# Where ScalarE's read of a finished MLP tile stands among the exponentials of its visit

## The chip, the cores and the metric

The kernel runs on one core of a Trainium2 chip. The metric is the device time of one execution in microseconds (us), and the median of several executions counts. The core has five engines with a queue of their own each: TensorE (PE in the profile, with PEld for its weight loads) for matrix products, VectorE (DVE), ScalarE (ACT), GpSimd (POOL), and SyncE (SP), which here starts the DMA transfers. Each engine takes its instructions in the order in which they were issued to it, and waits on semaphores for the others.

## The reference

One transformer-like block in fp32 with 2048 tokens, 512 features, 32 heads of 16 and an MLP of width 1792:

```python
xn = _layernorm(x, axis=-1)
qkv = (xn @ wqkv).reshape(B, S, 3, H, Dh).transpose(2, 0, 3, 1, 4)
scores = jnp.einsum("bhqd,bhkd->bhqk", q, k) * (Dh ** -0.5)
p = softmax(scores, axis=-1)
s = jnp.einsum("bhqk,bhkd->bhqd", p, v).transpose(0, 2, 1, 3).reshape(B, S, D) @ wo
h = jnp.einsum("bsd,df->bsf", xn, w1) + b1
r = jnp.where(h > 0, h, 0)
m = jnp.einsum("bsf,fd->bsd", r * r, w2) + b2
return x + s * silu(m)
```

## The kernel before

After a lead-in (layer norm, the q, k and v projections) the kernel runs one loop of 512 *steps*. A step is one unit (four heads, 512 queries; 32 units) and one block of 128 keys (16 a unit). For a step TensorE makes four score tiles `se` of 128x512, ScalarE takes the exponential of each (`exp_mm`, lines 1161 and 1167), and two steps later four matmuls multiply them with v into `po` (`pv_mm`, line 374). The softmax needs a maximum of each row beforehand; it comes from a second set of score matmuls (`max_mm`, line 300), whose tiles `pm_t` VectorE reduces (line 308).

Products with a contraction of 64 or less use half of TensorE's rows. The kernel therefore has two *lanes*: lane 0 is rows 0 to 63, lane 1 rows 64 to 127, and matmuls of different lanes run side by side. The score and maximum matmuls belong to one lane or the other; the v matmuls use all the rows and a quarter of the columns each.

The MLP and the projection by wo are spread over the steps as "dense" work, on TensorE by line 234 (`block`) or line 202 (`halves`). Each is a sum of matmuls, hi and lo parts of both factors, into one PSUM tile `pd_t`. There is a single buffer of that tile (pool `pd`, `bufs=1`). So the first matmul of the next dense tile waits until the last reader of this one is through: ScalarE's two `Relu` of 128x256 for a pair of first-layer tiles (`first_pair`, line 545), or ScalarE's copy of 128x512 to `u` for the second layer (`second`, line 566). This closing read is called `post` in the code. Behind the Relu, GpSimd squares and splits (lines 548, 80, 81).

Each long dense tile, a *block*, is laid over four steps by `long_slots`. Its sums are cut into 12 units "D" for each lane; a unit is two matmuls of 256 columns in the first layer (`per=2`, input `xc`, weights `w1s`) and one of 512 in the second (`w2t`, `hT`). First lane 0 does its 12 units (h = 0, two steps), then lane 1 (h = 1, two steps), and meanwhile the other lane makes maxima ("m") and scores ("s"). `visit(h, mine, theirs)` takes both strings letter by letter: `mine` is lane h, `theirs` the other lane. Where the maxima are far enough ahead (`ahead_m`), a half is a single visit of 14 letters, followed by the v matmuls of two steps. Otherwise the half is split: ten D beside `msmsmsmsms`, the v matmuls of one step, then the short closing visit, `DDss` beside `mmsm`, and the v matmuls of another step. `post` is called behind the last visit of h = 1.

The program built from this has 88 blocks. In 54, all in the earlier part, both halves are single visits; in 34, all in the later part, both are split. 55 blocks end in a `post` (49 pairs of Relu, 6 copies): 34 of single visits and 21 of split ones. Of the 34 split blocks 19 are of the first layer.

The order of the work on each engine is that of the Python calls (`manual_schedule`): nothing reorders it. One further dependency is written out by hand: `last_use` is the exponential of the first score tile of lane h behind the lane's last D; the other lane's first D waits for it (line 239), since both lanes add into the same `pd_t`. The score tiles rotate over three PSUM buffers (`pe`, `bufs=3`), the maxima over three (`pm`). GpSimd's tile `r` has two buffers.

Of the kernel before, what the change touches and what calls it, by code (L numbers as in the profile page):

```python
# [39 lines left out]
def kernel(  # L40
# [55 lines left out]
    with ExitStack() as ph:  # L96
# [191 lines left out]
        def max_mm(j, spread=False):  # L288
            if not m_ready(j, 1):
                return None  # L290
            u, p, qb, kc = todo_m[j].pop(0)
            qd = u // 4
            if u not in mxs:
                mxs[u] = sp.tile([P, 16, 4], F32, name="mx")
            m_bank[0] += 1
            if spread and m_bank[0] % 2:
                ps = pe.tile([P, 512], F32, name="se")
            else:
                ps = pm.tile([P, 512], F32, name="pm_t")
            nc.tensor.matmul(  # L300
                ps,
                qms[u][p][64 * j : 64 * j + 64, qb * P : (qb + 1) * P],
                kas[qd, p][64 * j : 64 * j + 64, kc * 512 : (kc + 1) * 512],
                start=True, stop=True,
            )
            c = (2 * p + j) * 4 + qb
            done_m[j] += 1
            return nc.vector.tensor_reduce(  # L308
                mxs[u][:, c, kc : kc + 1], ps, axis=AX.X, op=ALU.max
            )  # L310
# [3 lines left out]
        def max_end():  # L314
            while steps[0] < sum(done_m) // 4:
                u, s = divmod(steps[0], 16)
                if s == 15 and min(done_m) < 32 * (u + 1):
                    return
                steps[0] += 1
                if s in (9, 11) and u + 1 < NU:  # L320
                    assert min(done_m) >= 32 * u + 16
                    load_q_pair(u + 1, "qm", (s - 9) // 2, qms.setdefault(u + 1, []))
                if s == 15:
                    m4 = sp.tile([P, 16], F32, name="m4")
                    nc.vector.tensor_reduce(m4, mxs[u], axis=AX.X, op=ALU.max)
                    mxs[u] = m4
                    late.append((now[0] + 2, u))

        def shift_due():
            if late and late[0][0] <= now[0]:  # L330
                shift(late.pop(0)[1])
# [821 lines left out]
        def exp_mm(st, j, pts, spare):  # L1153
            u, kb = divmod(st, 16)
            qd = u // 4
            b = 64 * (j % 2)
            if spare:
                se = pm.tile([P, 512], F32, name="pm_t")
            else:
                se = pe.tile([P, 512], F32, name="se")  # L1160
            nc.tensor.matmul(  # L1161
                se, kas[qd, j // 2][b : b + 64, kb * P : (kb + 1) * P],
                qes[u][j // 2][b : b + 64, :],
                start=True, stop=True,
            )
            pts[j] = free_pt.pop(0)
            return nc.scalar.activation(pts[j], se, AF.Exp, scale=0.25)  # L1167
# [3 lines left out]
        def pv_step(st, pts):  # L1171
            u, kb = divmod(st, 16)
            if kb == 0:
                pos[0] = pv.tile([P, 512], F32, name="po")
            pv_mm(pos[0], u // 4, kb, pts)
            free_pt.extend(t for _, t in sorted(pts.items()) if all(t is not x for x in gone_pt))
            if kb == NT - 1:
                if u < NU - 2:
                    evac(pos[0], u)
                elif u == NU - 2:  # L1180
                    unit_inner(pos[0])
                else:
                    unit_final(pos[0])
# [57 lines left out]
        def ahead_m(n, st):  # L1241
            wo0 = 16 * NU - 62
            for u in range(n // 64, NU):
                end = 16 * u - SHIFT
                n_max = n + 4 * max(0, end - st)
                n_max += max(0, min(end, wo0 + 32) - max(st, wo0))
                if n_max < 64 * (u + 1):
                    return False
            return True

        def long_slots(st0, units, post):

            todo = [[(st0 + k, j) for k in range(4) for j in (lane, lane + 2)] for lane in range(2)]
            for kb in range(st0, st0 + 4):
                pts.setdefault(kb, {})

            def s(lane):
                kb, j = todo[lane].pop(0)
                return exp_mm(kb, j, pts[kb], False)

            def visit(h, mine, theirs):
                own, other, follow = units[h], 1 - h, True
                for i, ops in enumerate(zip(mine, theirs)):
                    for lane in (other, h):
                        o = ops[0] if lane == h else ops[1]
                        if o == "D":
                            own.pop(0)()
                        elif o == "m":
                            max_mm(lane)
                        elif o == "s":  # L1270
                            use = s(lane)
                            if lane == h and not own and follow:
                                last_use[0], follow = use, False

            for h in range(2):
                st = st0 + 2 * h
                if st > st0:
                    begin(st)
                if ahead_m(sum(done_m) + 7, st + 2):
                    visit(h, "s" + "D" * 12 + "s", ".mmsmssmsmssmm")  # L1280
                    if h and post is not None:
                        post()
                    begin(st + 1)
                    max_end()
                    shift_due()
                    for kb in (st - 2, st - 1):
                        pv_step(kb, pts.pop(kb))
                else:
                    visit(h, "D" * 10, "msmsmsmsms")
                    max_end()  # L1290
                    shift_due()
                    pv_step(st - 2, pts.pop(st - 2))
                    begin(st + 1)
                    visit(h, "DDss", "mmsm")
                    if h and post is not None:
                        post()
                    max_end()
                    shift_due()
                    pv_step(st - 1, pts.pop(st - 1))
            if post is not None:  # L1300
                last_use[0] = None
            assert not todo[0] and not todo[1] and not units[0] and not units[1]
# [17 lines left out]
        def begin(st):  # L1320
            now[0] = st
            if st % 64 == 48 and st // 64 + 1 < NQ:
                load_v(st // 64 + 1)
            if st >= 64 and st % 64 < 6 and st // 64 + 1 < NQ:
                for n in range(2):
                    load_k(st // 64 + 1, 2 * (st % 64) + n)
            u, s = divmod(st + 16, 16)
            if 2 <= u < NU and s < 2:
                load_q_pair(u, "qe", s, qes.setdefault(u, []))
            run_waiting()  # L1330

        done = 0
        for st_ in range(NU * 16):
            if st_ < done:
                continue
            begin(st_)
            if st_ < 2:
                slot(st_, [], None, 6)
                shift_due()
                continue  # L1340
            if st_ == 2:
                assert len(rest) == 1 and next(rest[0], None) is None
                qs.close()
            item = next(dn, None)
            if item is not None and len(item) > 2:
                assert st_ % 4 == 0
                long_slots(st_, *item[:2])
                done = st_ + 4
                continue
            if item is not None and item[0] is not None:  # L1350
                slot(st_, *item)
            else:
                plain_slot(st_)
            shift_due()
            if st_ > 1:
                pv_step(st_ - 2, pts.pop(st_ - 2))
# [30 lines left out]
```

## Time and profile before

| what | value |
|---|---|
| median of 3 runs | 1714.3 us (1711.1 to 1719.36) |
| profiled execution, its own time | 1710.34 us |
| span in its trace | 1708.6 us |
| granted TensorE clock | 0.998 |
| TensorE busy | 1655.0 us, 97% |
| VectorE busy | 1337.6 us, 78% |
| ScalarE busy | 1193.0 us, 70% |
| GpSimd busy | 528.9 us, 31% |

The profiled execution took 4.0 us less than the median, and its span is 1.7 us shorter than its own time. In the rows of a group, the first numbers behind the bar are busy time and mean length of one instruction, then the idle time of the engine just before them and who ended it. In a timeline a row has the start (us), the time it covers, the engine, the line and the operation, the output and the inputs, the number of instructions run together (x), and in brackets the idle time of the engine before it with its releaser. Rows run together overlap: three exponentials of 0.61 us each can cover 1.57 us. 64*128 64x512 is a matmul on 64 rows of TensorE (one lane) that streams 512 columns.

### The profile page before, as it was taken

The page shows a single profiled execution, that of the slowest core. Times are in us where ns is not written, and L with a number is a line of the kernel's source. Part 1 is how long each engine was busy: PE and PEld are TensorE (multiplying, and loading weights), DVE is VectorE, ACT ScalarE, POOL GpSimd, SP SyncE. Part 2 cuts the span into 40 slices and gives each one's busy share as a digit, 9 for nine tenths or more (in the row PEclk, how much of TensorE's full clock was granted, in tenths as well). Part 3 has the DMA queues.
Part 4 walks back from the last instruction along what each step waited for, and adds up shares of the span by engine and source line. Part 5 has one row for each costly group of instructions (what it writes and reads, how often), then busy time and mean ns, then how long its engine had stood idle before and what let it go on. Part 6 is the DMA issues. An engine that isn't in the chain of part 4 may idle for free.

```text
span 1708.6 us, 35413 instructions
## 1 busy us (share of the span) xinstructions
PE 1655.0 (97%) x13296; PEld 987.1 (58%) x13296; DVE 1337.6 (78%) x2294; ACT 1193.0 (70%) x2354; POOL 528.9 (31%) x548
## 2 busy tenths in 40 slices
PE   6999999999999999999999999999999999999997
PEld 5766666556656655665566565545554555555533
DVE  6599988887787787788787878888888888888612
ACT  6211377778777777787787777777777777766685
POOL 4434467513212221232032122212220223133333
PEclk9999999999999999999999999999999999999999
DMA  7567454436233522353144234242324332157344
GB/s 278 167 202 245 171 174 157 133 84 163 77 87 94 138 73 79 119 131 93 52 142 103 88 87 116 64 110 85 101 70 119 88 104 57 40 190 210 100 144 136
DMA packets 156723, 208.00 MB, mean 122 GB/s; under 512 B 51272, under 2 KB 71240, under 8 KB 155016
## 3 DMA queue, kind: packets, MB, share of 16 engines
q1 hardware_dynamic: 156552, 205.74, 41.5%
q8 instruction: 105, 1.72, 0.4%
q14 instruction: 66, 0.54, 0.1%
HBM read 149.30 MB, written 56.09 MB: 120 GB/s over the span
## 4 chain that ended last, share of the span: by engine, by line
PE 82%; issue 5%; ACT 3%; POOL 3%; DMA 3%; DVE 2%; SPq 1%; POOLq 0%; ACTq 0%; DVEq 0%
PE po L374 24%; PE pd_t L234 15%; PE pm_t L300 14%; PE se L1161 13%; PE pd_t L202 6%; PE pd_t L936 2%; PE po L936 2%; DVE mx L308 2%; ACT pt L1167 2%; PE se L300 2%; ACT r L545 1%; PE po L967 1%; PE pd_t L967 1%; POOL ts L751 1%; POOL ts L750 1%
## 5 line engine op out<-in xcount | busy, mean ns | idle before, releaser
L308 DVE TENSOR_REDUCE mx<-pm_t 128x1 f32<-128x512 f32 x1946 | 1209.5, 683 | 251.8 <-PE pm_t L300 156.5
L1167 ACT ACTIVATE pt<-se 128x512 f32<-128x512 f32 x1721 | 909.5, 612 | 283.3 <-PE se L1161 185.0
L1161 PE MATMUL se<-qe,ka 64*128 64x512 f32 x1988 | 761.3, 421 | 2.0 <-ACT ex L1167 1.0
L300 PE MATMUL pm_t<-ka,qm 64*128 64x512 f32 x1946 | 737.4, 416 | 3.5 <-DVE mx L308 2.4
L374 PE MATMUL po<-pt,v 128*32 128x512 f32 x3562 | 522.2, 602 | 0.0
L300 PEld LDWEIGHTS pm_t<-ka,qm 64*128 64x128 f32 x1946 | 341.3, 184 | 220.7 <-DVE mx L308 202.3
L1161 PEld LDWEIGHTS se<-qe,ka 64*128 64x128 f32 x1988 | 352.9, 184 | 129.3 <-ACT pt L1167 57.1
L234 PE MATMUL pd_t<-xc,w1s 64*128 64x256 f32 x2352 | 317.9, 285 | 12.5 <-ACT r L545 11.5
L234 PEld LDWEIGHTS pd_t<-xc,w1s 64*128 64x128 f32 x2352 | 296.5, 187 | 20.9 <-ACT r L545 16.5
L234 PE MATMUL pd_t<-w2t,hT 64*128 64x512 f32 x936 | 248.1, 402 | 2.4 <-ACT r L545 2.4
L374 PE MATMUL po<-ex,v 128*32 128x512 f32 x534 | 204.8, 601 | 0.0
L1167 ACT ACTIVATE ex<-se 128x512 f32<-128x512 f32 x267 | 158.1, 612 | 51.0 <-PE se L1161 25.8
L374 PEld LDWEIGHTS po<-pt,v 128*32 128x32 f32 x3562 | 90.7, 108 | 157.4 <-issue 140.2
L234 PEld LDWEIGHTS pd_t<-w2t,hT 64*128 64x128 f32 x936 | 162.5, 184 | 11.5 <-issue 3.3
L548 POOL TENSOR_TENSOR r<-r 128x512 f32<-128x512 f32 x49 | 51.0, 1040 | 354.2 <-ACT r L545 354.2
L567 POOL TENSOR_TENSOR u<-u,b_t 128x512 f32<-128x512 f32 x16 | 20.6, 1287 | 290.8 <-ACT u L566 290.8
L202 PE MATMUL pd_t<-w2t,hT 64*128 64x512 f32 x408 | 105.8, 391 | 0.1
L412 POOL TENSOR_TENSOR ot<-ot,hl 128x512 f32<-128x512 f32 x31 | 39.8, 1283 | 199.1 <-DMA hl<-r_d 167.5
L202 PE MATMUL pd_t<-wot,oc 64*128 64x512 f32 x336 | 90.9, 406 | 8.7 <-DVE mx L308 6.2
L202 PEld LDWEIGHTS pd_t<-wot,oc 64*128 64x128 f32 x336 | 58.4, 184 | 58.7 <-ACT pt L1167 16.0
L308 DVE TENSOR_REDUCE mx<-se 128x1 f32<-128x512 f32 x102 | 69.7, 683 | 14.7 <-PE se L300 8.7
L202 PEld LDWEIGHTS pd_t<-w2t,hT 64*128 64x128 f32 x408 | 72.5, 184 | 9.8 <-POOL w2t L81 0.5
(125 smaller groups left out, 1229.5 us busy)
## 6 DMA issues: line engine op xcount, KB each, us to landing
w1s<-w_d SPq DMA_DIRECT2D x196, 256.0 KB
qm<-q_d SPq DMA_DIRECT2D x384, 32.0 KB
qe<-q_d SPq DMA_DIRECT2D x384, 32.0 KB
ka<-k_d SPq DMA_DIRECT2D x96, 128.0 KB
xn_d<-xT SPq DMA_DIRECT2D x8, 1024.0 KB
k_d<-hl SPq DMA_DIRECT2D x32, 256.0 KB
q_d<-hl SPq DMA_DIRECT2D x32, 256.0 KB
xc<-xn_d SPq DMA_DIRECT2D x16, 512.0 KB
```

The costliest lines, as they stand in the source:

```text
L202: mm = nc.tensor.matmul(out_, lh(r), rh(r), start=first_ and lane == 0, stop=last_ and lane == 1, skip_group_check=True,)
L234: mm = nc.tensor.matmul(out_, lh(r), rh(r), start=first_ and lane == 0, stop=last_ and lane == 1, skip_group_check=True,)
L300: nc.tensor.matmul(ps, qms[u][p][64 * j : 64 * j + 64, qb * P : (qb + 1) * P], kas[qd, p][64 * j : 64 * j + 64, kc * 512 : (kc + 1) * 512] ...
L308: return nc.vector.tensor_reduce(mxs[u][:, c, kc : kc + 1], ps, axis=AX.X, op=ALU.max)
L374: nc.tensor.matmul(po[32 * j : 32 * j + 32, :], vs[qd][:, (4 * kb + j) * VW : (4 * kb + j) * VW + 32], pts[j], start=(kb == 0), stop=(kb = ...
L412: nc.gpsimd.tensor_tensor(ot, ot, hl[:, 1].bitcast(F32), op=ALU.mult)
L548: nc.gpsimd.tensor_tensor(r, r, r, op=ALU.mult)
L567: nc.gpsimd.tensor_tensor(u, u, b2_t, op=ALU.add)
L936: nc.tensor.matmul(out_, lh(slice(0, P)), rh(slice(0, P)), start=first_, stop=last_)
L967: nc.tensor.matmul(out_, lh(slice(0, P)), rh(slice(0, P)), start=first_, stop=last_)
L1161: nc.tensor.matmul(se, kas[qd, j // 2][b : b + 64, kb * P : (kb + 1) * P], qes[u][j // 2][b : b + 64, :], start=True, stop=True,)
L1167: return nc.scalar.activation(pts[j], se, AF.Exp, scale=0.25)
```

## The change

`visit` gets a flag that lets lane h go first at each letter, used for the short closing visit of both halves; and `post` is no longer called behind the visit but inside it, at the letter at which lane 1 has issued its last D.

```diff
-            def visit(h, mine, theirs):
+            def visit(h, mine, theirs, h_first=False):
                 own, other, follow = units[h], 1 - h, True
                 for i, ops in enumerate(zip(mine, theirs)):
-                    for lane in (other, h):
+                    for lane in (h, other) if h_first else (other, h):
                         o = ops[0] if lane == h else ops[1]
...
+                    if h and not units[h] and wrap:
+                        wrap.pop()()
+
+            wrap = [post] if post is not None else []
             for h in range(2):
...
                     visit(h, "s" + "D" * 12 + "s", ".mmsmssmsmssmm")
-                    if h and post is not None:
-                        post()
                     begin(st + 1)
...
-                    visit(h, "DDss", "mmsm")
-                    if h and post is not None:
-                        post()
+                    visit(h, "DDss", "mmsm", True)
                     max_end()
```

The number and the kind of instructions are the same. On VectorE, GpSimd and SyncE no instruction moves; on TensorE and ScalarE some do. TensorE, the closing visit of h = 1 of a split first-layer block, from the v matmuls to the v matmuls; `ka0` with `qm0` is a maximum of the other lane, `se` a score tile. Before:

```order
L374 MATMUL po_19006<-pt4_1345,v0_1437 32x512
L300 MATMUL pm_t_19378<-ka0_203,qm0_200 128x512
L234 MATMUL pd_t_19225<-xc_17586,w1s3_2323 128x256 x2
L300 MATMUL pm_t_19383<-ka0_203,qm0_200 128x512
L234 MATMUL pd_t_19225<-xc_17586,w1s3_2323 128x256 x2
L1161 MATMUL se_19389<-qe3_689,ka1_204 128x512
L1161 MATMUL se_19392<-qe2_688,ka0_203 128x512
L300 MATMUL pm_t_19395<-ka0_203,qm0_200 128x512
L1161 MATMUL se_19398<-qe3_689,ka1_204 128x512
L374 MATMUL po_19006<-pt7_1348,v0_1437 32x512
```

The same visit with the change:

```order
L374 MATMUL po_19006<-pt7_1348,v0_1437 32x512
L234 MATMUL pd_t_19225<-xc_17586,w1s3_2323 128x256 x2
L300 MATMUL pm_t_19380<-ka0_203,qm0_200 128x512
L234 MATMUL pd_t_19225<-xc_17586,w1s3_2323 128x256 x2
L300 MATMUL pm_t_19386<-ka0_203,qm0_200 128x512
L1161 MATMUL se_19394<-qe2_688,ka0_203 128x512
L1161 MATMUL se_19397<-qe3_689,ka1_204 128x512
L1161 MATMUL se_19400<-qe3_689,ka1_204 128x512
L300 MATMUL pm_t_19403<-ka0_203,qm0_200 128x512
L374 MATMUL po_19006<-pt0_1341,v0_1437 32x512
```

Each pair of letters has changed places: D now stands ahead of the maximum beside it, and the lane's own score ahead of the other's. This happens in the closing visits of both halves of the 34 split blocks, 68 in all. ScalarE, the end of the same block; `r1<-pd_t_19225` are the two Relu that read it, `se_19416` is the first score tile of the next block. Before:

```order
L1167 ACTIVATE pt6_1347<-se_19365 128x512
L1167 ACTIVATE pt5_1346<-se_19389 128x512
L1167 ACTIVATE pt8_1349<-se_19392 128x512
L1167 ACTIVATE pt1_1342<-se_19398 128x512
L545 ACTIVATE r1_2312<-pd_t_19225,b1_t_148 128x256 x2
L1167 ACTIVATE pt11_1352<-se_19416 128x512
```

With the change:

```order
L1167 ACTIVATE pt10_1351<-se_19365 128x512
L545 ACTIVATE r1_2312<-pd_t_19225,b1_t_148 128x256 x2
L1167 ACTIVATE pt1_1342<-se_19394 128x512
L1167 ACTIVATE pt4_1345<-se_19397 128x512
L1167 ACTIVATE ex0_2305<-se_19400 128x512
L1167 ACTIVATE pt9_1350<-se_19416 128x512
```

The Relu pair has moved ahead of the three exponentials of the closing visit. In a block of single visits it moves ahead of one, and TensorE's order stays. ScalarE at the end of such a block, before:

```order
L1167 ACTIVATE pt6_1347<-se_7994 128x512
L1167 ACTIVATE pt12_1353<-se_8008 128x512
L545 ACTIVATE r0_2311<-pd_t_7855,b1_t_148 128x256 x2
L1167 ACTIVATE pt7_1348<-se_8029 128x512
L1167 ACTIVATE ex1_2306<-se_8042 128x512
```

With the change:

```order
L1167 ACTIVATE pt6_1347<-se_7994 128x512
L545 ACTIVATE r0_2311<-pd_t_7855,b1_t_148 128x256 x2
L1167 ACTIVATE pt12_1353<-se_8013 128x512
L1167 ACTIVATE pt7_1348<-se_8029 128x512
L1167 ACTIVATE ex1_2306<-se_8042 128x512
```

Only the exponential of the visit's last letter has changed sides with the Relu pair.

## The prediction

> **What bounds the kernel now.** I read the page first: the span, the engines and the chain of work that ended last.
>
> ```profile
> span 1708.6 us, 35413 instructions
> ...
> PE 1655.0 (97%) x13296; PEld 987.1 (58%) x13296; DVE 1337.6 (78%) x2294; ACT 1193.0 (70%) x2354; POOL 528.9 (31%) x548
> ...
> PE 82%; issue 5%; ACT 3%; POOL 3%; DMA 3%; DVE 2%; SPq 1%; POOLq 0%; ACTq 0%; DVEq 0%
> ```
>
> TensorE carries the end, so what an edit on ScalarE is worth is what it takes out of TensorE's waits. The view of the waits for TensorE alone has two rows on the first matmul of a dense tile, and the view of the groups tells which kind of D waited.
>
> ```profile
> PE pd_t L234 <- ACT r L545: 13.9, 19, 0.8
> ...
> PE pd_t L234 <- ACT u L566: 1.0, 2, 0.5
> ```
>
> ```profile
> L234 PE MATMUL pd_t<-xc,w1s 64*128 64x256 f32 x2352 | 317.9, 285 | 12.5 <-ACT r L545 11.5 <-ACT u L566 1.0
> ...
> L234 PE MATMUL pd_t<-w2t,hT 64*128 64x512 f32 x936 | 248.1, 402 | 2.4 <-ACT r L545 2.4
> ```
>
> Those are 19 + 2 = 21 waits, exactly the number of split blocks that end in a read; the 34 reads behind single visits have none. The groups divide them: 11.5 us of 0.72 each are 16 waits of a first-layer D for the Relu, 2.4 of 0.81 are 3 of a second-layer D, and 1.0 are the two for the copy (one wait of each size stands below). The 14.9 us that the two rows add up to are only the part in which TensorE did nothing at all; the timeline around one of them shows what a wait costs. First the end of a split block with its closing visit and the next block's first half, then, without a read ahead of it, that block's second half:
>
> ```profile
> 1200.39 0.49 PE L300 MATMUL pm_t<-ka,qm 64*128 64x512 f32 x1
> 1200.39 0.50 PE L234 MATMUL pd_t<-xc,w1s 64*128 64x256 f32 x2
> ...
> 1200.73 0.40 PE L234 MATMUL pd_t<-xc,w1s 64*128 64x256 f32 x2
> ...
> 1200.92 1.89 DVE L308 TENSOR_REDUCE mx<-pm_t 128x1 f32<-128x512 f32 x3 [0.50 <-PE pd_t L234]
> 1200.96 0.41 PE L1161 MATMUL se<-qe,ka 64*128 64x512 f32 x2
> ...
> 1201.19 0.32 SPq L468 DMA_DIRECT2D w1s<-w_d  x1
> ...
> 1201.39 1.57 ACT L1167 ACTIVATE pt<-se 128x512 f32<-128x512 f32 x3 [1.23 <-PE se L1161]
> ...
> 1201.53 1.07 PE L374 MATMUL po<-pt,v 128*32 128x512 f32 x8
> ...
> 1202.52 0.50 PE L300 MATMUL pm_t<-ka,qm 64*128 64x512 f32 x1
> 1202.83 0.85 ACT L545 ACTIVATE r<-pd_t,b_t 128x256 f32<-128x256 f32 x2
> ...
> 1203.74 0.38 PE L234 MATMUL pd_t<-xc,w1s 64*128 64x256 f32 x1 [0.72 <-ACT r L545]
> ...
> 1203.84 0.46 PE L1161 MATMUL se<-qe,ka 64*128 64x512 f32 x1
> ...
> 1206.32 0.62 PE L374 MATMUL po<-pt,v 128*32 128x512 f32 x2
> ...
> 1209.45 0.50 PE L234 MATMUL pd_t<-xc,w1s 64*128 64x256 f32 x2
> ...
> 1209.79 0.39 PE L1161 MATMUL se<-qe,ka 64*128 64x512 f32 x1
> ...
> 1209.98 3.08 DVE L308 TENSOR_REDUCE mx<-pm_t 128x1 f32<-128x512 f32 x5 [0.25 <-PE pm_t L300]
> ...
> 1210.71 0.39 PE L1161 MATMUL se<-qe,ka 64*128 64x512 f32 x1
> ...
> 1212.02 1.06 PE L374 MATMUL po<-pt,v 128*32 128x512 f32 x8
> ```
>
> The three exponentials start at 1201.39 behind 1.23 us of idling, then come the two Relu, which end at 1202.83 + 0.85 = 1203.68; the next block's first D starts 0.06 later, at 1203.74. Its visit had begun at 1202.52 with the other lane's maximum. Nothing behind that D in TensorE's queue could start, so the visit stood for 1203.74 - 1202.52 = **1.22 us**. From D to the v matmuls the visit then takes 1206.32 - 1203.74 = 2.58 us; in the half without a read it takes 1212.02 - 1209.45 = 2.57. Hence the wait isn't made up later: it lengthens the block by itself.
>
> **Part one: the read moves ahead of the exponentials, in split blocks.** The last D of the visit ends at 1200.73 + 0.40 = 1201.13. ScalarE has been idle since 1201.39 - 1.23 = 1200.16. With the change the Relu pair starts at about 1201.19 (the same 0.06 for the hand-over), takes 0.85 and ends at 1202.04. TensorE can't come to the next D before 1202.52. So the read is ready 0.48 us early and the whole wait goes. This is the first of the three kinds, with 16 waits. The other two, each with the start of its visit and the D:
>
> ```profile
> 1253.40 0.50 PE L300 MATMUL pm_t<-ka,qm 64*128 64x512 f32 x1
> ...
> 1254.71 0.47 PE L234 MATMUL pd_t<-w2t,hT 64*128 64x512 f32 x1 [0.81 <-ACT r L545]
> ```
>
> ```profile
> 1164.48 0.50 PE L300 MATMUL pm_t<-ka,qm 64*128 64x512 f32 x1
> ...
> 1165.47 0.38 PE L234 MATMUL pd_t<-xc,w1s 64*128 64x256 f32 x1 [0.50 <-ACT u L566]
> ```
>
> They cost 1.31 and 0.99. Sum: 16 x 1.22 + 3 x 1.31 + 2 x 0.99 = 19.5 + 3.9 + 2.0 = **25.4 us**.
>
> What is late next? The three exponentials now start at 1202.04 and end at 1203.61. Their score buffers are wanted by the next visit's scores: in the half without a wait these start 0.34 behind the visit's start (1209.79 - 1209.45) and then 0.46 apart ((1210.71 - 1209.79) / 2). From 1202.52 that is 1202.86, 1203.32 and 1203.78. The three exponentials, some 0.5 apart and 0.6 long, are through at about 1202.65, 1203.1 and 1203.6: 0.2 us to spare each time. I charge nothing; without this margin each lacking tenth would cost 21 x 0.1 = 2.1 us. The maxima do not come to bind either: in the half without a read VectorE idles 0.25 before its five reductions, waiting for TensorE. The transfer of weights issued at 1201.19 is for the block after the next (eight buffers, four a block), which can't begin before the second half at 1209.45: 8 us of slack.
>
> **Part two: the read moves ahead of one exponential, in blocks of single visits.** One such end, with the half before it, which has no read:
>
> ```profile
> 544.77 0.63 PE L374 MATMUL po<-pt,v 128*32 128x512 f32 x3
> ...
> 546.62 0.49 PE L1161 MATMUL se<-qe,ka 64*128 64x512 f32 x1
> ```
>
> ```profile
> 549.66 0.40 PE L234 MATMUL pd_t<-xc,w1s 64*128 64x256 f32 x2
> ...
> 550.23 1.92 PE L374 MATMUL po<-pt,v 128*32 128x512 f32 x16
> ...
> 550.57 0.66 ACT L1167 ACTIVATE pt<-se 128x512 f32<-128x512 f32 x1
> ...
> 551.04 0.90 ACT L545 ACTIVATE r<-pd_t,b_t 128x256 f32<-128x256 f32 x2
> ...
> 552.09 0.49 PE L1161 MATMUL se<-qe,ka 64*128 64x512 f32 x1
> ...
> 553.12 0.39 PE L1161 MATMUL se<-qe,ka 64*128 64x512 f32 x1
> ```
>
> Sixteen v matmuls lie between the last D and the next block. They take 552.09 - 550.23 = 1.86 us with a read in this time and 546.62 - 544.77 = 1.85 without, so the read, over at 551.94, is hidden and there is nothing to gain. The displaced exponential ends some 0.9 later than before, near 552.1. Its buffer is wanted by the third score of the next block, at 553.12. The margin is 1.0 us, and the cost of these 34 moves is nothing; without the margin it would be up to 0.9 each.
>
> **Part three: lane h goes first in 68 closing visits.** A first-layer D is two matmuls in one lane, and the other lane's maximum now stands behind both. Rows that show such an order are those where a block starts with D after a wait; the program has D, D, score there:
>
> ```profile
> 1412.08 0.38 PE L234 MATMUL pd_t<-xc,w1s 64*128 64x256 f32 x1 [0.71 <-ACT r L545]
> ...
> 1412.08 0.50 PE L1161 MATMUL se<-qe,ka 64*128 64x512 f32 x1
> ...
> 1412.30 0.40 PE L234 MATMUL pd_t<-xc,w1s 64*128 64x256 f32 x2
> ```
>
> The other lane's score starts with the first D, 0.22 ahead of the second, which it follows in the program: a lane doesn't wait for the other's second matmul. At the other start shown the score came 0.10 behind the D (1203.84 against 1203.74), still ahead of its second matmul. So a visit loses between 0 and 0.10, 0 to 6.8 us over 68; a gain is excluded, since no matmul is taken away. As most such starts look like the one at 1412, I take 0.02 a visit: 1.4 us.
>
> The Trainium skill says the opposite: TensorE: Matmul & The Clock Gate, section Part 3 (packing small matmuls), has matmuls start and end strictly in the order of the program, with only weight loads pulled ahead. This trace's 1412.08 against 1412.30 disagrees. By that rule the sum would be that of the first rival below.
>
> Sum: 25.4 - 1.4 = 24.0. The profiled execution took 1710.3 us, 1.7 over its span, and would take 1686.3. The median of the runs stands 4.0 above it, and on that footing the forecast is 1714.3 - 24.0 = **1690.3, said as 1690**.
>
> **The rivals.**
>
> *The two lanes start strictly in program order.* Then in the 38 closing visits of the 19 first-layer split blocks the maximum starts 0.22 late (1412.08 to 1412.30). The other lane's first matmul has 0.34 before the next starts (1200.39 to 1200.73) and the later ones 0.23, so 0.22 + 0.23 - 0.34 = 0.11 stays: 38 x 0.11 = 4.2 us. Gain 25.4 - 4.2 = 21.2, time 1693. For it: the rule just named, and that the waiting itself holds the other lane back (nothing starts between 1202.52 and 1203.74). Against: the rows at 1412.
>
> *The wait moves to the exponentials.* If the Relu pair starts only when it would have found the first score done (1201.39) and loses another 0.4 between the engines, the exponentials are 0.6 late, 0.4 beyond the margin, at every one of the 21 ends: 21 x 0.4 = 8.4. Gain 25.4 - 1.4 - 8.4 = 15.6, time 1699. For it: the margin is 0.2. Against: ScalarE idles over 1 us there.
>
> *Slower: the closing visit loses its pairing.* If the maximum of the other lane waits until both matmuls of the D beside it are through (0.50 in the row at 1200.39), and the second-layer visits lose as much, 68 x 0.50 = 34 us are lost against 25.4: 8.6 slower, 1723. It decides from 25.4 / 68 = 0.37 a visit. Against it again the rows at 1412.
>
> *The change does not do what it says:* another release, of a weight buffer or a maximum's, ends just behind the read and holds the same D. Then some 1712. Against: 0.06 from the read's end to the D, and the halves without a read that start D at once.
>
> **How the numbers follow.** Forecast 0.68, strict order 0.16, wait moved 0.08, no effect 0.05, slower 0.03. A measurement of this kernel tells about 0.5%, 8.6 us, from no change. The first three cases are faster than that: 0.92. No effect lies within: 0.05; the last is slower: 0.03. The low end is the full 25.4 taken from the lowest run shown, 1711.1, less the spread of some 3 us between runs: 1683. The high end takes in strict order and a moved wait, and the same spread: 1702. That leaves out the last two cases and the edges of the others, under 2 in 10.
>
> **What would show it.** The two rows of TensorE's waits on the read go, and the 21 first D stand beside the visit's first maximum. ScalarE's idle 1.23 before the three exponentials becomes a wait for the last D ahead of the Relu. In the earlier part, as long as blocks are single visits, no time changes. Wrong would be: score matmuls that wait for exponentials right behind those block ends (wait moved); maxima in closing visits 0.2 behind their D and v matmuls 0.1 later (strict order); a first D that still starts over a microsecond behind its visit.

## The result, and the profile after

The change takes the median from 1714.57 us (4 runs, 1711.1 to 1719.36) to 1686.84 us (4 runs, 1685.38 to 1688.89). The ratio is 0.9837 with a 95% interval of 0.9811 to 0.9864, so 23 to 32 us are gained. The forecast was 1690, with a gain of 24.0. In the trace the span went from 1708.6 to 1684.1 us, by 24.5.

The page of the profile after, its span, its engines and the chain that ended last:

```profile
span 1684.1 us, 35351 instructions
...
PE 1645.7 (98%) x13296; PEld 980.9 (58%) x13296; DVE 1334.7 (79%) x2294; ACT 1190.0 (71%) x2354; POOL 529.2 (31%) x548
...
PE 84%; issue 5%; POOL 4%; DMA 3%; DVE 2%; SPq 1%; ACT 1%; POOLq 0%; ACTq 0%
```

ScalarE's share of the chain has fallen from 3% to 1%; each engine in the second row ran as many instructions as before. The view of TensorE's waits after, its longest rows:

```profile
PE pm_t L1010 <- ACT xn L1003: 14.3, 9, 6.4
PE pd_t L202 <- DVE mx L308: 6.2, 19, 0.4
PE pm_t L300 <- DVE mx L308: 2.7, 6, 1.1
```

The two rows of line 234 are gone: 13.9 us for the Relu and 1.0 for the copy. What stands first is a wait of the lead-in that was there before (14.1 us). The groups after, the D matmuls and the Relu, and behind them the Relu's row before:

```profile
L234 PE MATMUL pd_t<-xc,w1s 64*128 64x256 f32 x2352 | 318.0, 285 | 0.0
L234 PE MATMUL pd_t<-w2t,hT 64*128 64x512 f32 x936 | 249.0, 403 | 0.0
...
L545 ACT ACTIVATE r<-pd_t,b_t 128x256 f32<-128x256 f32 x98 | 42.6, 506 | 20.4 <-PE pd_t L234 20.4
```

```profile
L545 ACT ACTIVATE r<-pd_t,b_t 128x256 f32<-128x256 f32 x98 | 43.2, 524 | 0.0
```

The waiting has changed sides. Before, D waited for the Relu, and the Relu never for D; now no D waits, and ScalarE idles 20.4 us for the last D ahead of its Relu. The timeline after, the end of the same block that the prediction shows:

```profile
1191.26 0.38 PE L234 MATMUL pd_t<-xc,w1s 64*128 64x256 f32 x1
...
1191.27 0.50 PE L300 MATMUL pm_t<-ka,qm 64*128 64x512 f32 x1
...
1191.49 0.40 PE L234 MATMUL pd_t<-xc,w1s 64*128 64x256 f32 x2
...
1191.73 0.28 PE L234 MATMUL pd_t<-xc,w1s 64*128 64x256 f32 x1
...
1192.10 0.84 ACT L545 ACTIVATE r<-pd_t,b_t 128x256 f32<-128x256 f32 x2 [1.09 <-PE pd_t L234]
...
1192.39 0.63 PE L374 MATMUL po<-pt,v 128*32 128x512 f32 x3
...
1192.83 1.57 ACT L1167 ACTIVATE pt<-se 128x512 f32<-128x512 f32 x3
...
1193.39 0.50 PE L300 MATMUL pm_t<-ka,qm 64*128 64x512 f32 x1
...
1193.39 0.50 PE L234 MATMUL pd_t<-xc,w1s 64*128 64x256 f32 x2
...
1193.72 0.39 PE L1161 MATMUL se<-qe,ka 64*128 64x512 f32 x1
...
1193.96 0.39 PE L300 MATMUL pm_t<-ka,qm 64*128 64x512 f32 x1
```

The last D ends at 1191.73 + 0.28 = 1192.01, the Relu pair runs from 1192.10 to 1192.94, and the next block's first D stands beside its maximum at 1193.39, 0.45 behind the end of the read. The three exponentials begin behind the Relu and delay nobody.

To leave the lead-in out of the comparison I took two copies to `u` that neither kernel moves (they belong to short tasks that are not blocks), one ahead of all the 21 split ends and one behind them. Between them lie 1464.4 - 958.3 = 506.1 us before and 1439.7 - 959.2 = 480.5 after: 25.6 us less. Of that 0.5 belongs to an end of single visits that also lies there (next paragraph), which leaves 25.1, or 1.20 for each of the 21.

Two more rows of TensorE's waits before are gone, which the prediction does not speak of:

```profile
PE se L1161 <- ACT ex L1167: 1.0, 2, 0.5
PE se L1161 <- ACT pt L1167: 1.0, 2, 0.5
```

They are four waits of a score matmul for an exponential, one behind each of the four copies to `u` that close a block of single visits. One of them before, from the first score of the next block on, and the same place after:

```profile
529.06 0.50 PE L1161 MATMUL se<-qe,ka 64*128 64x512 f32 x1
...
530.08 0.63 ACT L572 ACTIVATE r<-u 128x512 f32<-128x512 f32 x1 [1.40 <-POOL u L567]
...
531.25 0.50 PE L1161 MATMUL se<-qe,ka 64*128 64x512 f32 x1 [0.50 <-ACT pt L1167]
```

```profile
530.66 0.50 PE L1161 MATMUL se<-qe,ka 64*128 64x512 f32 x1
...
531.19 0.63 ACT L572 ACTIVATE r<-u 128x512 f32<-128x512 f32 x1 [0.90 <-POOL u L567]
...
532.36 0.49 PE L1161 MATMUL se<-qe,ka 64*128 64x512 f32 x1
```

GpSimd adds a bias to the copy (line 567), ScalarE's next instruction on it (line 572) waits for that sum, and the next block's exponentials stand behind that instruction in ScalarE's queue. With the copy ahead of one more exponential this instruction starts 0.53 us behind the block's first score and not 1.02, and the fourth score comes at 1.70 and not 2.19. So 0.49 us is won at each of four ends, 2.0 us in all. Behind a Relu the fourth score comes at 1.26 in both traces; the 0.44 us that are left behind each of the four copies no run here tried to win.

### The profile page after: what moved, and what is told of

It reads as the page before. It is cut to its first block, busy times and chain, and to the rows that moved or that the text cites. A ratio compares the mean times of both kernels' runs of the same rounds, so it can differ in the third digit from the quotient of the medians.

```text
span 1684.1 us, 35351 instructions
## 1 busy us (share of the span) xinstructions
PE 1645.7 (98%) x13296; PEld 980.9 (58%) x13296; DVE 1334.7 (79%) x2294; ACT 1190.0 (71%) x2354; POOL 529.2 (31%) x548
## 4 chain that ended last, share of the span: by engine, by line
PE 84%; issue 5%; POOL 4%; DMA 3%; DVE 2%; SPq 1%; ACT 1%; POOLq 0%; ACTq 0%
PE po L374 26%; PE pd_t L234 16%; PE se L1161 14%; PE pm_t L300 13%; PE pd_t L202 5%; PE pd_t L936 2%; PE po L936 2%; DVE mx L308 2%; PE se L300 2%; PE po L967 1%; PE pd_t L967 1%; DMA hl<-r_d 1%; POOL ts L751 1%; POOL ts L750 1%; PE se L936 1%
## 5 line engine op out<-in xcount | busy, mean ns | idle before, releaser
L234 PEld LDWEIGHTS pd_t<-w2t,hT 64*128 64x128 f32 x936 | 162.4, 185 | 33.9 <-issue 25.1
```

Source lines behind the costliest of these rows:

```text
L234: mm = nc.tensor.matmul(out_, lh(r), rh(r), start=first_ and lane == 0, stop=last_ and lane == 1, skip_group_check=True,)
```

## The experiments

All ran beside the kernel before (medians there 1712.6 and 1712.9 us). Each gets the difference of its edit from the change.

**The read early, the lanes in their old order.**

```diff
-                    visit(h, "DDss", "mmsm", True)
+                    visit(h, "DDss", "mmsm")
```

> The read is issued behind the last D as in the change, but both lanes keep the old order in the closing visits (the other lane first). My theory: the last D ends at the same place, the read starts as early, all 21 waits go: 25.4 us gained, about 1688 against 1714, the same as the change within 2. Rival, the lanes start strictly in program order: without the new order 4.2 us more are gained than with it, about 1683. Rival, the new order is what brings the read early enough: some of the 21 waits stay, over 1695.

Measured: 1686.99 us, ratio 0.985 (0.9833 to 0.9867), as good as the change. The trace shows no wait of a D for a read; the Relu starts 0.86 us behind the start of the closing visit (with the new order 0.84). Early reading alone makes the gain; the first rival's 1683 lies outside the interval of 1684 to 1690, though only just.

**The new order, the read behind the visit.**

```diff
-                    if h and not units[h] and wrap:
-                        wrap.pop()()
...
                     visit(h, "DDss", "mmsm", True)
+                    if h and wrap:
+                        wrap.pop()()
```

(the same behind the 14-letter visit)

> Lane h goes first in the 68 closing visits, but the read stays behind the visit, after the three exponentials. My theory: the order costs nearly nothing (0 to 1.4 us) and gains nothing, and all 21 waits of about 1.2 us are still there: 1714 to 1716. Rival, strict program order: 4.2 us slower than before, about 1719. Rival, the visits lose their pairing: 34 us slower, 1748. Rival, the order itself brought the gain: about 1690.

Measured: 1714.1 us, ratio 1.0005 (0.9994 to 1.0017): the order costs between -1.0 and 2.9 us. TensorE's waits in this run, and its timeline at the start of a block:

```profile
PE pd_t L234 <- ACT r L545: 14.4, 19, 0.8
```

```profile
1190.96 0.50 PE L300 MATMUL pm_t<-ka,qm 64*128 64x512 f32 x1
1191.30 0.85 ACT L545 ACTIVATE r<-pd_t,b_t 128x256 f32<-128x256 f32 x2
...
1192.20 0.38 PE L234 MATMUL pd_t<-xc,w1s 64*128 64x256 f32 x1 [0.74 <-ACT r L545]
```

The waits are all back, the 16 of this kind with 1192.20 - 1190.96 = 1.24 us each, and so are the four waits of a score behind the copies. Strict order (4.2 us) and a lost pairing (34 us) are both outside the interval.

**The read early in single visits alone.**

```diff
-                    if h and not units[h] and wrap:
+                    if h and not units[h] and wrap and len(mine) == 14:
                         wrap.pop()()
...
-                    visit(h, "DDss", "mmsm", True)
+                    visit(h, "DDss", "mmsm")
+                    if h and wrap:
+                        wrap.pop()()
```

> The read moves ahead of one exponential in the 34 blocks of single visits alone; the 21 split ends are as before. My theory: the sixteen v matmuls hid that read before, so nothing is gained and nothing lost: 1714 within 3, and 21 waits remain. Rival, part of the gain comes from the single visits: under 1709. Rival, the late exponential starves the score buffers: up to 34 x 0.9 = 31 us slower, 1745.

Measured: 1711.85 us, ratio 0.9995 (0.9983 to 1.0007). The time shows no gain and no loss that can be told (-2.9 to 1.2 us), with the split ends' waits in place:

```profile
PE pd_t L234 <- ACT r L545: 13.9, 19, 0.8
...
PE pd_t L234 <- ACT u L566: 1.0, 2, 0.5
```

The trace is finer than the time here. The four waits of a score are not in it. Two copies to `u` that no edit moves enclose one of those four ends, in the part of the single visits. Between them lie 804.92 - 649.78 = 155.1 us in this run and 803.83 - 648.60 = 155.2 with the change, against 802.49 - 646.77 = 155.7 in the kernel before and 803.54 - 647.87 = 155.7 with the new order alone. So reading early in the single visits wins 0.5 us where a copy closes the block, and the four together are 2.0 us, inside what the time leaves open.

**The read one and two exponentials later.** If the read's place sets the time, each exponential put ahead of it must cost a fixed amount, from the point where the read's end passes the next D.

```diff
                             use = s(lane)
+                            if h and h_first and wrap:
+                                held[0] += 1
+                                if held[0] == 1:
+                                    wrap.pop()()
...
-                    if h and not units[h] and wrap:
+                    if h and not units[h] and wrap and not h_first:
```

(`held` starts at 0 in every block; the second kernel has 2 in place of 1)

> As the change, but in split closing visits the read stands behind the first of the three exponentials. My theory counts in steps of one exponential, 0.48 us: the Relu pair would end about 0.2 after the next D could start, so each of the 19 Relu ends waits some 0.27 us with the hand-over and the two copies hardly: 5 us given back, about 1692, and about 19 waits in the trace with a delay of 0.2 to 0.3 us from visit start to D. Rival, any place ahead of the last exponential is as good: 1687. Rival, the read only helps at the very first place: most of the gain lost, over 1705.

> As the change, but in split closing visits the read stands behind the second of the three exponentials. Measured behind the first: 1692.0, 5 us over the change, as forecast. My theory goes on by 0.48 us for each exponential: 0.75 us of wait at the 19 Relu ends and 0.5 at the two copies, 15 us given back, about 1702. Rival, the loss saturates (the first exponential was the whole of it): about 1692. Rival, all is lost as soon as the read is late by more than the hand-over: 1712.

Measured: 1692.0 us (ratio 0.9878, 0.9859 to 0.9896) and 1699.38 us (0.9921, 0.9903 to 0.994). Behind one exponential, the end of a block:

```profile
1192.90 0.60 ACT L1167 ACTIVATE pt<-se 128x512 f32<-128x512 f32 x1 [1.27 <-PE se L1161]
...
1193.40 0.83 ACT L545 ACTIVATE r<-pd_t,b_t 128x256 f32<-128x256 f32 x2
...
1194.02 0.49 PE L300 MATMUL pm_t<-ka,qm 64*128 64x512 f32 x1
...
1194.28 0.38 PE L234 MATMUL pd_t<-xc,w1s 64*128 64x256 f32 x1
```

Behind two:

```profile
1196.02 0.84 ACT L545 ACTIVATE r<-pd_t,b_t 128x256 f32<-128x256 f32 x2
...
1196.16 0.49 PE L300 MATMUL pm_t<-ka,qm 64*128 64x512 f32 x1
...
1196.91 0.38 PE L234 MATMUL pd_t<-xc,w1s 64*128 64x256 f32 x1 [0.26 <-ACT r L545]
```

D is late by 1194.28 - 1194.02 = 0.26 and by 1196.91 - 1196.16 = 0.75 us; with the read behind all three it was 1.22. That is one exponential (0.48) at a time, as worked out ahead. The first kernel's row shows no idle time although D is 0.26 late, and the second's shows 0.26 of 0.75: the maximum beside D counts as TensorE's work for about 0.5 us, and hides that much of each wait from the idle column. The times follow: 1686.8, 1692.0, 1699.4 and, before, 1712.6. The second gave back 12.5 us where I expected 15; between the two copies its trace does show 1453.1 - 956.2 = 496.9 us, 16.4 more than the change. Its lead-in, the time up to the first copy, is 3.0 us shorter than the change's (956.2 against 959.2), so the shortfall is of the size by which executions differ.

**The exponentials later, the read in place.** One and two more Relu on the SBUF tile r, which free the PSUM tile no later but stand ahead of the exponentials (the diff has the first kernel; the second runs the added line twice):

```diff
                             r[:, i], ps[:, i * CW : (i + 1) * CW], AF.Relu, bias=b1_t[:, fo : fo + 1]
                         )
+                    nc.scalar.activation(r[:, 1], r[:, 1], AF.Relu)
```

> As the change, with one more Relu of 128x256 on the SBUF tile r behind the pair in the first-layer blocks (a second Relu changes no value); it does not read the PSUM tile, so the next D is free as before, and the exponentials behind it are some 0.4 us later. My theory: the exponentials have 0.2 to 0.3 us to spare before the next visit's scores need their buffers, so 0.1 to 0.2 is lost at each of the 19 split ends: 2 to 4 us, 1689 to 1691; the single visits have 1 us to spare and lose nothing. Rival, the exponentials have no part in the end: 1687. Rival, there is no margin, the wait had already moved to them: 8 us, 1695.

> The same with two such Relu, the exponentials some 0.8 us later. My theory: 0.5 to 0.6 beyond the margin at each of the 19 split ends, 10 to 11 us: 1697 to 1698, and still nothing in single visits. Rival, no part in the end: 1687. Rival, no margin: 16 us, 1703; with the single visits also out of their margin: over 1710.

Measured: 1690.16 us (ratio 0.9862, 0.9845 to 0.988) and 1700.41 us (0.9925, 0.9909 to 0.9941). The added lines shift the numbers: in the first kernel 1162 is the score matmul; in the second 549 is the added Relu, 1163 the score matmul, 1169 the exponential. In the second the view of TensorE's waits has rows on the score matmuls behind the 19 split Relu ends, where neither kernel had any, and the timeline shows one of them:

```profile
PE se L1163 <- ACT pt L1169: 8.1, 17, 0.5
...
PE se L1163 <- ACT ex L1169: 1.0, 2, 0.5
```

```profile
1199.87 0.87 ACT L549 ACTIVATE r<-r 128x256 f32<-128x256 f32 x2
...
1200.29 0.50 PE L234 MATMUL pd_t<-xc,w1s 64*128 64x256 f32 x2
1200.64 1.55 ACT L1169 ACTIVATE pt<-se 128x512 f32<-128x512 f32 x3
...
1201.27 0.50 PE L1163 MATMUL se<-qe,ka 64*128 64x512 f32 x1 [0.48 <-ACT pt L1169]
...
1201.61 0.39 PE L300 MATMUL pm_t<-ka,qm 64*128 64x512 f32 x1
```

D is on time, but the score behind it comes at 0.98 in place of 0.33 us (1201.27 - 1200.29 against 1193.72 - 1193.39), and the next maximum at 1.32 in place of 0.57: 0.75 us at each of 19 ends, 14.2 us, and 13.6 were measured. I had expected 0.5 to 0.6 each. The first kernel, with one Relu more, at the start of a block:

```profile
1192.78 0.50 PE L300 MATMUL pm_t<-ka,qm 64*128 64x512 f32 x1
...
1193.33 0.49 PE L1162 MATMUL se<-qe,ka 64*128 64x512 f32 x1
```

The score comes at 0.55 in place of 0.33, so 0.42 us more on ScalarE make it 0.22 late: the margin of 0.2 that the forecast relied on is real and small. What lies beyond it costs more than I expected here too. A split block takes 11.75 us in this trace (Relu at 1191.50 and 1203.25), 0.35 over the change, where I had expected 0.1 to 0.2. At 19 ends that is 6.7 us, and the medians differ by only 3.3: most of this trace's first-layer blocks of single visits take 10.85 us in place of 10.95, which makes up part of it. For that I have no cause, and that the time came out within the expected 1689 to 1691 is luck.

**The split blocks made single visits, the read early.** A try at a kernel faster than both.

```diff
-                    visit(h, "D" * 10, "msmsmsmsms")
-                    max_end()
-                    shift_due()
-                    pv_step(st - 2, pts.pop(st - 2))
-                    begin(st + 1)
-                    visit(h, "DDss", "mmsm", True)
+                    visit(h, "D" * 12 + "ss", "msmsmsmsmsmmsm")
+                    begin(st + 1)
                     max_end()
                     shift_due()
-                    pv_step(st - 1, pts.pop(st - 1))
+                    for kb in (st - 2, st - 1):
+                        pv_step(kb, pts.pop(kb))
```

> The read early as in the change, and the 34 split blocks made single visits of 14 letters with all eight maxima (DDDDDDDDDDDDss beside msmsmsmsmsmmsm), the v matmuls of two steps behind. A split block now takes 11.4 us in the trace, one of single visits 10.95: 0.45 for the second switch. My theory: eight maxima in one visit wait for VectorE (0.6 us each, three buffers), by 0.3 to 0.5 us a half, more than the switch costs: 1690 to 1705, slower than the change. Rival, VectorE catches up during the v matmuls and the switch is saved: 34 x 0.45 = 15 us faster, about 1672.

Measured: 1704.29 us, ratio 0.9947 (0.9931 to 0.9963): 17 us slower than the change. The timeline of one half:

```profile
1203.21 0.50 PE L300 MATMUL pm_t<-ka,qm 64*128 64x512 f32 x1
...
1203.74 4.88 DVE L308 TENSOR_REDUCE mx<-pm_t 128x1 f32<-128x512 f32 x8 [1.08 <-PE pd_t L234]
...
1205.68 0.50 PE L300 MATMUL pm_t<-ka,qm 64*128 64x512 f32 x1
...
1206.28 0.50 PE L300 MATMUL pm_t<-ka,qm 64*128 64x512 f32 x1
...
1206.88 0.50 PE L300 MATMUL pm_t<-ka,qm 64*128 64x512 f32 x1
...
1209.16 0.50 PE L300 MATMUL pm_t<-ka,qm 64*128 64x512 f32 x1
```

VectorE works through all eight reductions without a gap, and the last three maxima come 0.60 apart, its pace (4.88 / 8 = 0.61) and not TensorE's, whose maxima come 0.47 apart earlier in the same half. The half takes 1209.16 - 1203.21 = 5.95 us. Split, with the read early, a block takes 11.40 us (Relu at 1192.10 and 1203.50), 5.70 a half. So 68 x 0.25 = 17 us are lost, as much as was measured. In a split half the v matmuls in the middle give VectorE the time to catch up: in the trace after it idles 0.54 us ahead of its three reductions and 0.20 ahead of its five. So the split stays. No kernel beat the change.

## Why the prediction was right

*The bound.* That TensorE carries the end held, and its waits for the read were nearly all that could be won; 2.0 us more lay in four waits of its scores.

*The wait, 25.4 us.* Right in place, number and size. The 21 waits are gone, and the stretch that holds them is 25.6 us shorter, 25.1 of it at these ends. The read behind three, two, one and no exponential makes D 1.22, 0.75, 0.26 and 0 us late, and the time goes with it.

*What is late next.* Nothing was; the margins named were there. Relu was to start 0.80 behind the start of its visit and started at 0.84. The exponentials' margin of 0.2 was tested from its far side: once it is used up, the price appears where it was expected, at the next visit's scores: they are 0.22 us late with 0.42 more on ScalarE and 0.65 with 0.87 more. What I expected in those two runs beyond the margin was too small, since a stop of TensorE inside a visit costs more than its length: behind it the next matmul of the lane comes 0.34 us later and not 0.24 (1201.61 - 1201.27 against 1193.96 - 1193.72).

*Single visits, nothing.* Right for the 30 that end in a Relu, and not for the four that end in a copy: the prediction read one Relu end and took it for all 34, and put at nothing what gained 4 x 0.49 = 2.0 us. The next D is no earlier there, as it said; what comes earlier is ScalarE's own next instruction on the copy, and with it the exponentials. The time alone (0.9995 when the single visits alone are changed) can't tell 2.0 us from nothing; the traces do.

*The order of the lanes, 1.4 us.* The other term that was mis-sized: it is nothing that can be told. The closing visit takes 1192.39 - 1191.26 = 1.13 us in the new order and took 1.14 in the old one, and with the read early the two orders give 1686.84 and 1686.99. Strict order of the starts does not hold for two lanes here: the maximum at 1191.27 starts 0.22 ahead of the second D matmul at 1191.49 that it follows in the program, in a visit that no wait had stopped, and the order alone changed the time by less than the 4.2 us that strict order would cost. The Trainium skill states that strict order (TensorE: Matmul & The Clock Gate, section Part 3). For the starts, this trace disagrees with it.

*The whole.* 24.0 forecast and 27.7 between the medians, with an interval of 23 to 32. Of the difference 1.4 is the order's term and 2.0 the four waits behind the copies; with both set right the sum is 27.4. The interval is too wide to confirm a sum that closely. The forecast's two wrong terms are both small, and neither is the read's wait on which it rests. The rivals are all out: the wait didn't move to the exponentials, no second release stood behind the read, and the visits kept their pairing.

## What to carry to other kernels

Where one buffer is filled and read in turn, issue its reader directly behind the last write, ahead of anything on the reader's engine that nobody waits for yet; what that is worth is the time by which the next writer is late against the same place without a read, not the idle time that a wait's row shows. Work moved behind the read has a margin of its own, and it is found the same way: when is its buffer wanted next? Where other work already covers the read, as sixteen v matmuls do here, the next writer gains nothing by it; then ask what the reader's own engine waits for behind it. At four ends here that was worth 0.49 us each.

## What the runs showed that I had not expected

A stop of TensorE inside a visit costs about 0.1 us over its length, since the pair of matmuls behind it takes 0.34 us and not 0.23 to 0.24 (in the run with two Relu more, 0.75 for a score that is 0.65 late); at 19 ends that is 2 us. And the idle column of TensorE can be empty while its queue stands: a first D late by 0.26 us showed no idle time, because the one matmul of the other lane that had started counts as work for 0.5 us.
